# Streaming the activations instead of the second weight matrix in an RWKV-and-FFN kernel

## The chip, the cores and the metric

The kernel runs on one core of one Trainium2 chip. Its time is the device time of one execution in microseconds (us). The metric is the median over the runs; lower is better. All engines of the core take part: TensorE (PE) multiplies, VectorE (DVE), ScalarE (ACT) and GpSimd (POOL) work element by element, and SyncE (SP) issues the transfers between DRAM and the core's memory SBUF. A matmul has a stationary operand of 128 rows and up to 128 columns, which a weight load (PEld) puts into the array, and a moving operand, whose columns stream past it; the result falls into an accumulator bank of PSUM, 128 partitions by 512 float32.

## What is computed

An attention-like recurrence with a state of 48 by 48 for each of 4 batches and 8 heads, over 768 tokens, is followed by a feed-forward layer: 3072 tokens of 384 numbers times `w_in` (384 by 2048), an ELU, and times `w_out` (2048 by 384).

```python
def _attn_ref(r, k, v, w, u):            # B, H, S, D = 4, 8, 768, 48
    state = np.zeros((B, H, D, D))
    for t in range(S):
        kt, vt, rt = (k[:, :, t], v[:, :, t], r[:, :, t])
        cur = np.einsum('bhd,bhe->bhde', u[None] * kt, vt)
        y[:, :, t] = np.einsum('bhd,bhde->bhe', rt, state + cur)
        state = w[None, :, :, None] * state + np.einsum('bhd,bhe->bhde', kt, vt)
    return y

def _moe_ref(x, w_in, w_out):
    h = x @ w_in
    g = np.where(h > 0.0, h, 1.0 * (np.exp(np.minimum(h, 0.0)) - 1.0))
    return (g @ w_out).astype(np.float32)
```

`reference` runs the first on `r, k, v, w, u`, lays the result out as 3072 rows (batch times token) of 384, and runs the second on it.

## The kernel before

The 768 tokens are cut into six blocks of 128 (`NCH`); a block of the feed-forward layer is the 128 tokens of all four batches, 512 columns (`T`). The 2048 hidden channels are cut into 16 groups of 128 (`NF`). A **step** (n, f) is one block and one group, so there are 96 of them, and `step` issues for each, in the order of the tables `FIRST` (block 0) and `LATER` (the others):

- `hidden` (L1172): nine matmuls of 512 columns, three 128-row pieces of x times three products. Both operands are split into a high and a low part (`xh`, `xl`, `wh`, `wl`), and high-high, high-low and low-high are summed.
- `negative`, `elu`, `split_g` (L1181 to L1195): two activations on ACT, one operation on DVE, a rounding copy on ACT for the high part of g, and a subtraction on DVE for the low part.
- `project` (L1209) for the step two before: g is the stationary operand, one 128 by 128 piece for each batch, and 384 columns of `w_out` stream past it. That is four batches times three products, twelve matmuls, into four accumulators `acc0` to `acc3` (one bank each, one buffer each), which collect the 16 groups of a block.

PE takes its work in the order it is written: `hidden` of this step, some small matmuls of the attention in two steps of four, then `project` of the step two before. The attention of the next block runs in units of one batch, spread over four steps each, beside the feed-forward work of this block. In block 0 the weights are also prepared, step by step (ACT, DVE, and `rest_w` L611 on POOL).

When `project` has finished the last group of a block, `store` runs at the end of that step, which is step f = 1 of the next block. It empties the four accumulators, batches 0 and 2 on ACT (L1224), 1 and 3 on DVE (L1222), into the tile `o` (it lies in the weights' old staging area, so the trace calls it `stage`), and issues four stores of 192 KB on the SP queue (L1226). On DVE the copies stand behind that step's `elu` (L1187), low part (L1195) and reduction (L727). The next block's first `project`, in the following step, may write an accumulator only when its copy has ended.

On the SP queue, which is served in order, a unit has four transfers of turned blocks to DRAM (L641), their way back (L646), the loads of r, k and v (L155, L159), and six small transfers that fill rows of x (L1091). The blocks come from `turn_blocks` (L632), which turns 128 by 512 elements on DVE in pieces of 32 by 32.

The whole schedule is written by hand; nothing reorders it.

Of the kernel before, what the change touches and what calls it, by code (L numbers as in the profile page):

```python
# [8 lines left out]
F32 = mybir.dt.float32  # L9
# [8 lines left out]
P = 128  # L18
B, H, S, D = 4, 8, 768, 48
# [3 lines left out]
NC = DM // P  # L23
NF = DFF // P
NCH = S // P
T = B * P
# [30 lines left out]
class Kernel:  # L57
# [237 lines left out]
    def start(self):  # L295
        nc = self.nc

        t = self.wk.tile([P, 2, X // 2], F32, tag="x", name="raw", bufs=2)
        for b in (2, 3):
            n, at = H * DP, t[:, b - 2, :]  # L300
            self.raw[0, b] = [
                at[:, i * n : (i + 1) * n].rearrange("p (h d) -> p h d", h=H) for i in range(3)
            ]
            self.clear_pads(self.raw[0, b])
        self.begun, self.done = [], set()
        n = 3 * H * DP
        self.tails = [
            t[:, i, n : n + DM].rearrange("p (i c d) -> p i c d", i=2, c=NC) for i in range(2)
        ]
        a = self.wk.tile([P, T], F32, tag="a", name="vd", bufs=1)  # L310
        self.vds = [
            t.rearrange("p (c i d) -> p c i d", c=NC, i=2)
            for t in (a[:, 0:DM], self.wide[:, 0].bitcast(F32))
        ]
        for t in self.tails:
            nc.gpsimd.memset(t[:, :, :, 0:D], 0.0)
        dve = nc.vector
        ops = {
            "ub": lambda b: self.u_by_tokens(),
            "inv": lambda b: self.inverse_table(),  # L320
            "kt": lambda b: self.inverse_by_tokens(),
            "wm": lambda b: self.keep_warm(b),
            "Tr": lambda b: self.turn_in(0, b, "r"),
            "Tk": lambda b: self.turn_in(0, b, "k"),
            "dr": lambda b: self.decay_r(0, b),
            "dk": lambda b: self.decay_k(0, b),
            "A": lambda b: self.scores(0, b),
            "ru": lambda b: self.current(0, b),
            "sum": lambda b: self.current_sum(0, b),
            "Lr": lambda b: self.load_rk(0, b, (0,)),  # L330
            "Lk": lambda b: self.load_rk(0, b, (1,)),
            "Ln": lambda b: self.load_next(b),
            "tk": lambda b: self.take_k(0, b, dve.tensor_copy),
            "tka": lambda b: self.take_k(0, b, nc.scalar.copy),
            "uw": lambda b: self.current_by_channels(),
            "p": lambda b: self.current_turned(0, b, dve),
            "pp": lambda b: self.current_turned(0, b, nc.gpsimd),
            "q": lambda b: self.current_by_pe(0, b),
            "qa": lambda b: self.take_current(0, b, nc.scalar.copy),
            "qd": lambda b: self.take_current(0, b, dve.tensor_copy),  # L340
            "ht": lambda b: self.half_tables(),
            "tl": lambda b: self.copy_tails(0, b, nc.gpsimd.tensor_copy),
            "tla": lambda b: self.copy_tails(0, b, nc.scalar.copy),
            "tld": lambda b: self.copy_tails(0, b, dve.tensor_copy),
            "Lv": lambda b: self.load_v(0, b),
            "Lw": lambda b: self.load_weights(b),
            "kr": lambda b: self.key_rest(0, b),
            "krd": lambda b: self.key_rest(0, b, dve),
            "m0": lambda b: self.mask_scores(0, b, 0),
            "m1": lambda b: self.mask_scores(0, b, 1),  # L350
            "m0a": lambda b: self.mask_scores(0, b, 0, True),
            "m1a": lambda b: self.mask_scores(0, b, 1, True),
            "vd": lambda b: self.current_by_v(0, b),
            "vdd": lambda b: self.current_by_v(0, b, dve),
            "O": lambda b: self.output_by_channels(0, b),
            "V": lambda b: self.output_of_current(0, b),
            "xh": lambda b: self.split_output(0, b, 0),
            "xl": lambda b: self.split_output(0, b, 1),
            "dra": lambda b: self.decay_r(0, b, True),
            "dka": lambda b: self.decay_k(0, b, True),  # L360
            "rud": lambda b: self.current(0, b, dve),
            "rsd": lambda b: self.rest_w((b + 1) // 2, (b + 1) % 2, dve),
            "S": lambda b: self.first_state(b),
            "wd": lambda b: self.widen(b),
            "lb": lambda b: self.low_bits(b),
            "ma": lambda b: self.merge(b),
            "mb": lambda b: self.sign(b),
            "sp": lambda b: self.split_w(b),
            "rs": lambda b: self.rest_w((b + 1) // 2, (b + 1) % 2),
            "H": lambda b: self.hidden_half(b),  # L370
        }
        for op in START.split():
            name, _, b = op.partition(":")
            ops[name](int(b or 0))
        self.all_banks = False
# [16 lines left out]
    def step(self, n, f):  # L392
# [64 lines left out]
        for op in (LATER if n else FIRST).split():  # L457
# [3 lines left out]
            name, stage = op[:-1], int(op[-1], 16)  # L461
# [5 lines left out]
                    todo[name](m, b)  # L467
        if last[1] == NF - 1 and last[0] in self.acc:
            self.store(last[0])
        if (n, f) == (0, NF - 1):  # L470

            o = self.late.bitcast(F32).rearrange("p s d w -> p (s d w)")[:, 0 : B * DM]
            self.o = o.rearrange("p (b d) -> p b d", b=B)
# [715 lines left out]
    def split_g(self, n, f, i):  # L1189
# [5 lines left out]
            nc.vector.tensor_sub(part, g, self.g[n, f][2].bitcast(F32))  # L1195
        self.g[n, f].append(part)

    def project(self, n, f):
        gh, gl = self.g.pop((n, f))[2:]
        wh, wl = self.weight(f + 1, 0)  # L1200
        if f == 0:
            self.acc[n] = [
                self.ps.tile([P, 512], F32, tag=f"acc{b}", name=f"ps_acc{b}", bufs=1)
                for b in range(B)
            ]
        for b in range(B):
            at = slice(b * P, (b + 1) * P)
            for i, (a, w) in enumerate(((gh, wh), (gh, wl), (gl, wh))):
                self.nc.tensor.matmul(  # L1209
                    self.acc[n][b][:, 0:DM], lhsT=a[:, at], rhs=w,  # L1210
                    start=(f == 0 and i == 0), stop=(f == NF - 1 and i == 2),
                )

    def store(self, n):
        nc = self.nc
        for b, po in enumerate(self.acc.pop(n)):
            if self.general:
                o = self.wk.tile([P, DM], F32, tag="o", name="o", bufs=2)
            else:
                o = self.o[:, b, :]  # L1220
            if b % 2:
                nc.vector.tensor_copy(o, po[:, 0:DM])  # L1222
            else:
                nc.scalar.copy(o, po[:, 0:DM])  # L1224
            row = b * S + n * P
            nc.sync.dma_start(self.out[row : row + P, :], o)  # L1226
# [43 lines left out]
```

## Time and profile before

| | |
|---|---|
| median of 3 runs | 508.0 us |
| lowest and highest | 507.6 and 509.15 us |
| the profiled execution | 509.15 us, of which the span of the trace is 507.4 us |
| PE, share of the span busy | 97% |
| DVE, ACT, POOL | 56%, 51%, 30% |
| DMA engines, mean rate | 101 GB/s, 39.9% of their time |

The profiled execution is one of the three runs, and the slowest of them. A busy PE is not PE at its peak: each matmul's row lasts until its result is out, and the next one starts before that. So the cost of a matmul in a row of them is the distance from its start to the next start, not the length of its row, and the rows below are read by their starts.

### The profile page before, as it was taken

To read this page: it belongs to the slowest core of one execution; us is meant where nothing else is said; L and a number is where in the kernel's file an instruction comes from. 1 tells how busy PE (TensorE), PEld (TensorE's weight loads), DVE (VectorE), ACT (ScalarE), POOL (GpSimd) and SP (SyncE) were. 2 spreads that over 40 slices of the span, in tenths; PEclk is the share of its full clock that TensorE was granted. 3 is DMA by queue.
4 is the path that set the end of the run, shared out by engine and by line. 5 is a ranking of instruction groups with operands and counts; after the bars stand their busy time and mean duration, and the time that the engine had idled before them with its cause. 6 is when DMAs were issued, how large, how long until landed. Compare 5 with 4: busy or idle time off the path is not lost.

```text
span 507.4 us, 12065 instructions
## 1 busy us (share of the span) xinstructions
PE 491.5 (97%) x4900; PEld 433.4 (85%) x4900; DVE 285.0 (56%) x500; ACT 256.4 (51%) x448; POOL 154.5 (30%) x170
## 2 busy tenths in 40 slices
PE   9899999999999999999999999999999999999994
PEld 7788778888878888888888888888888989999994
DVE  5988989995564454554554653653644533433331
ACT  1458788864544444544444445445435435444441
POOL 3556768683222322312303303313212201000000
PEclk9999999999999999999999999999999999999999
DMA  8986685844533424453423434424443200100002
GB/s 154 236 173 158 154 221 141 178 107 98 166 79 96 123 60 97 107 136 91 113 66 93 122 106 112 110 58 110 102 119 104 76 17 10 62 1 1 1 0 70
DMA packets 105157, 51.10 MB, mean 101 GB/s; under 512 B 79746, under 2 KB 100996, under 8 KB 105092
## 3 DMA queue, kind: packets, MB, share of 16 engines
q1 hardware_dynamic: 105092, 50.23, 39.9%
q8 instruction: 41, 0.67, 0.6%
q14 instruction: 24, 0.20, 0.1%
HBM read 35.13 MB, written 13.11 MB: 95 GB/s over the span
## 4 chain that ended last, share of the span: by engine, by line
PE 75%; POOL 5%; SPq 5%; DMA 5%; DVE 4%; ACT 3%; issue 2%; DVEq 0%; ACTq 0%; POOLq 0%
PE ps_acc L1209 33%; PE ps_h L1172 32%; POOL wl L611 3%; PE ps_y L984 2%; PE ps_a L906 2%; PE ps_y L992 2%; PE ps_a L920 2%; SPq L1091 1%; SPq L201 1%; DMA stage<-in_moe_w_out_dram 1%; POOL k_t L734 1%; DMA raw<-in_v_dram 1%; DVE ps_h L1187 1%; DMA stage<-in_moe_w_in_dram 1%; DMA v_t<-in_v_dram 1%
## 5 line engine op out<-in xcount | busy, mean ns | idle before, releaser
L1209 PE MATMUL ps_acc<-wh,g 128*128 128x384 f32 x768 | 217.1, 343 | 0.4 <-DVE stage L1222 0.2
L1172 PE MATMUL ps_h<-x,wh 128*128 128x512 f32 (+1 forms) x588 | 180.3, 388 | 0.3 <-issue 0.2
L1209 PEld LDWEIGHTS ps_acc<-wh,g 128*128 128x128 f32 x768 | 140.1, 187 | 6.6 <-DVE stage L1222 1.3
L1209 PE MATMUL ps_acc<-wl,g 128*128 128x384 f32 x384 | 129.1, 336 | 0.0
L1187 DVE SCALAR_TENSOR_TENSOR ps_h<-g,ps_h 128x512 f32<-128x512 f32 x96 | 66.6, 694 | 100.8 <-ACT g L1182 100.8
L1172 PEld LDWEIGHTS ps_h<-x,wh 128*128 128x128 f32 x588 | 108.1, 188 | 17.3 <-issue 0.5
L1172 PE MATMUL ps_h<-x,wl 128*128 128x512 f32 (+1 forms) x294 | 115.0, 391 | 2.9 <-POOL wl L611 2.9
L1181 ACT ACTIVATE g<-ps_h 128x512 f32<-128x512 f32 x96 | 57.7, 601 | 87.6 <-PE ps_h L1172 87.5
L1193 ACT CAST g<-ps_h 128x512 fp32r<-128x512 f32 x96 | 56.3, 587 | 75.5 <-DVE ps_h L1187 75.2
L1195 DVE TENSOR_TENSOR g<-ps_h,g 128x512 fp32r<-128x512 f32 x96 | 66.2, 690 | 45.5 <-ACT g L1193 45.1
L1209 PEld LDWEIGHTS ps_acc<-wl,g 128*128 128x128 f32 x384 | 72.1, 188 | 2.1
L1172 PEld LDWEIGHTS ps_h<-x,wl 128*128 128x128 f32 x294 | 55.2, 188 | 16.7 <-POOL wl L611 5.3
L1182 ACT ACTIVATE g<-g 128x512 f32<-128x512 f32 x96 | 60.7, 632 | 3.1
L734 POOL TENSOR_TENSOR k_t<-k_t,rev 128x384 f32<-128x384 f32 x22 | 24.9, 1133 | 103.7 <-DVE ru L716 96.2
L1021 POOL TENSOR_TENSOR x<-x_f,x 128x512 fp32r<-128x512 f32 x16 | 20.7, 1296 | 91.5 <-ACT x L1019 91.5
L611 POOL TENSOR_TENSOR wl<-wide,wh 128x384 fp32r<-128x384 f32 x30 | 37.0, 1250 | 17.7 <-ACT wh L604 14.8
L968 DVE COPY_PREDICATED a<-mask,ps_a 128x256 f32<-128x256 int32 x40 | 17.8, 445 | 33.8 <-PE ps_a L920 32.9
L1003 ACT COPY x_f<-ps_y 128x256 f32<-128x256 f32 x40 | 12.9, 374 | 43.7 <-PE ps_y L992 43.7
L655 POOL TENSOR_TENSOR rk<-rk,pw 128x512 f32<-128x512 f32 x16 | 19.0, 1189 | 36.4 <-DMA rk<-blocks 36.4
L961 POOL TENSOR_TENSOR a<-ident_h,diag 128x512 f32<-128x512 f32 x20 | 21.6, 1080 | 6.7 <-DVE diag L727 5.3
L1012 DVE TENSOR_TENSOR x_f<-x_f,ps_y 128x128 f32<-128x128 f32 x40 | 9.7, 283 | 22.3 <-ACT x_f L1003 22.2
L586 DVE SCALAR_TENSOR_TENSOR wide<-stage 128x768 int32<-128x768 int32 (+1 forms) x17 | 21.5, 1262 | 0.1
(121 smaller groups left out, 416.4 us busy)
## 6 DMA issues: line engine op xcount, KB each, us to landing
blocks<-tb SPq DMA_DIRECT2D x64, 128.0 KB, 2.3
rk<-blocks SPq DMA_DIRECT2D x16, 512.0 KB, 3.5
stage<-in_moe_w_out_dram SPq DMA_DIRECT2D x16, 384.0 KB, 3.9
stage<-in_moe_w_in_dram SPq DMA_DIRECT2D x32, 144.0 KB, 3.8
out_dram<-stage SPq DMA_DIRECT2D x24, 192.0 KB, 2.0
r_t<-in_r_dram SPq DMA_DIRECT2D x22, 192.0 KB, 3.0
k_t<-in_k_dram SPq DMA_DIRECT2D x22, 192.0 KB, 3.6
v_t<-in_v_dram SPq DMA_DIRECT2D x22, 192.0 KB, 4.2
```

Source lines behind the costliest of these rows:

```text
L586: self.nc.vector.scalar_tensor_tensor(self.place(self.wide, k, WIDE), high, 3, low, op0=ALU.logical_shift_left, op1=ALU.bitwise_or,)
L611: (eng or self.nc.gpsimd).tensor_sub(lo, a, hi.bitcast(F32))
L734: (eng or self.nc.gpsimd).tensor_mul(k, k, self.rev[:, :, 0:D])
L961: self.nc.gpsimd.tensor_mul(un["a"], self.ident_h.unsqueeze(1).to_broadcast([P, H, DP]), un["diag"].unsqueeze(2).to_broadcast([P, H, DP]),)
L1021: (eng or nc.gpsimd).tensor_sub(x[:, 1], xf, x[:, 0].bitcast(F32))
L1172: self.nc.tensor.matmul(ph[:, part], lhsT=a[:, c * P : (c + 1) * P], rhs=x[:, c, part], start=(c == 0 and i == 0), stop=(c == NC - 1 and i ...
L1181: nc.scalar.activation(g, ph, AF.Relu, scale=-1.0)
L1182: nc.scalar.activation(g, g, AF.Exp, scale=-1.0)
L1187: self.nc.vector.scalar_tensor_tensor(ph, g, -1.0, ph, op0=ALU.add, op1=ALU.max)
L1193: nc.scalar.copy(part, g)
L1195: nc.vector.tensor_sub(part, g, self.g[n, f][2].bitcast(F32))
L1209: self.nc.tensor.matmul(self.acc[n][b][:, 0:DM], lhsT=a[:, at], rhs=w, start=(f == 0 and i == 0), stop=(f == NF - 1 and i == 2),)
```

## The change

For all blocks but the last (`by_rows`) `project` calls `project_turned`. There `w_out` is the stationary operand and g the moving one: 128 columns of `w_out`, every third one beginning at column c (`w[:, c::NC]`, so that neighbouring elements lie 12 bytes apart), for c = 0, 1, 2, and 512 columns of g. That is three column sets times three products, nine matmuls, into three accumulators, and the result is turned: channels on the partitions, tokens along the bank.

`store` calls `store_turned`: three instructions on DVE turn a bank each, 128 by 512, in blocks of 32 by 32, and write every third element of `o`. ACT has no part in it. After that a partition of `o` holds, for each of 16 groups of 32 tokens, 96 neighbouring channels of one token. The four stores become 16, of 48 KB each in runs of 384 bytes; they are put on a list, and every step issues two from it at its end (`store_pending`), from the step of `store` on. The last block is projected and stored as before.

```diff
+    def by_rows(self, n):
+        return self.general or n + 1 == NCH
+
     def project(self, n, f):
         gh, gl = self.g.pop((n, f))[2:]
         wh, wl = self.weight(f + 1, 0)
+        if not self.by_rows(n):
+            self.project_turned(n, f, gh, gl, wh, wl)
+            return
...
+    def project_turned(self, n, f, gh, gl, wh, wl):
+        if f == 0:
+            self.acc[n] = [
+                self.ps.tile([P, T], F32, tag=f"acc{c}", name=f"ps_acc{c}", bufs=1)
+                for c in range(NC)
+            ]
+        for c in range(NC):
+            for i, (w, g) in enumerate(((wh, gh), (wl, gh), (wh, gl))):
+                self.nc.tensor.matmul(
+                    self.acc[n][c], lhsT=w[:, c::NC], rhs=g,
+                    start=(f == 0 and i == 0), stop=(f == NF - 1 and i == 2),
+                )
+
+    def store_turned(self, n):
+        o = self.o.rearrange("p b d -> p (b d)").rearrange("p (t d c) -> p t d c", t=16, c=NC)
+        for c, po in enumerate(self.acc.pop(n)):
+            self.nc.vector.transpose(o[..., c], po.rearrange("p (t d) -> p t d", t=16))
+        rows = self.out.rearrange("(b n t p) (q d) -> b n t q p d", b=B, n=NCH, p=32, q=4)
+        self.pending = [(rows[b, n, t], o[:, b * 4 + t]) for b in range(B) for t in range(4)]
+
+    def store_pending(self, times):
+        for _ in range(min(times, len(self.pending))):
+            dst, src = self.pending.pop(0)
+            self.nc.sync.dma_start(dst, src.rearrange("p d c -> p (d c)"))
```

On PE, `project` of one step in block 1, before. In the names, `wh5` and `wl5` are the high and low part of a weight group, `g_0` and `g_1` the high and low part of g; the operand behind the arrow's comma is the stationary one:

```order
L1209 MATMUL ps_acc0_1798<-wh5_147,g_0_1964 128x384
L1209 MATMUL ps_acc0_1798<-wl5_148,g_0_1964 128x384
L1209 MATMUL ps_acc0_1798<-wh5_147,g_1_1972 128x384
L1209 MATMUL ps_acc1_1799<-wh5_147,g_0_1964 128x384
L1209 MATMUL ps_acc1_1799<-wl5_148,g_0_1964 128x384
L1209 MATMUL ps_acc1_1799<-wh5_147,g_1_1972 128x384
L1209 MATMUL ps_acc2_1800<-wh5_147,g_0_1964 128x384
L1209 MATMUL ps_acc2_1800<-wl5_148,g_0_1964 128x384
L1209 MATMUL ps_acc2_1800<-wh5_147,g_1_1972 128x384
L1209 MATMUL ps_acc3_1801<-wh5_147,g_0_1964 128x384
L1209 MATMUL ps_acc3_1801<-wl5_148,g_0_1964 128x384
L1209 MATMUL ps_acc3_1801<-wh5_147,g_1_1972 128x384
```

The same on PE in the changed kernel, for the group before it (`wh4`):

```order
L1229 MATMUL ps_acc0_1746<-g_0_1848,wh4_145 128x512
L1229 MATMUL ps_acc0_1746<-g_0_1848,wl4_146 128x512
L1229 MATMUL ps_acc0_1746<-g_1_1851,wh4_145 128x512
L1229 MATMUL ps_acc1_1747<-g_0_1848,wh4_145 128x512
L1229 MATMUL ps_acc1_1747<-g_0_1848,wl4_146 128x512
L1229 MATMUL ps_acc1_1747<-g_1_1851,wh4_145 128x512
L1229 MATMUL ps_acc2_1748<-g_0_1848,wh4_145 128x512
L1229 MATMUL ps_acc2_1748<-g_0_1848,wl4_146 128x512
L1229 MATMUL ps_acc2_1748<-g_1_1851,wh4_145 128x512
```

Twelve matmuls of 384 columns became nine of 512, 4608 columns either way, and the two operands changed sides.

On DVE, around the end of block 1, before: the last turns of attention blocks, an attention addition, `elu`, the low part of g, the reduction, and the two copies of the accumulators.

```order
L632 STREAM_TRANSPOSE tb<-k_t_70 128x4x4x32
L1012 TENSOR_TENSOR x_f<-x_f,ps_y 128x2x64 x2
L1187 SCALAR_TENSOR_TENSOR ps_h<-g,ps_h 128x512
L1195 TENSOR_TENSOR g_2744<-ps_h,g_2734 128x512
L727 TENSOR_REDUCE diag<-ru 128x4x2
L1222 COPY stage<-ps_acc_1799 128x384
L1222 COPY stage<-ps_acc_1801 128x384
L1187 SCALAR_TENSOR_TENSOR ps_h<-g,ps_h 128x512
L1195 TENSOR_TENSOR g_2798<-ps_h,g_2796 128x512
```

The same place on DVE in the changed kernel:

```order
L633 STREAM_TRANSPOSE tb<-k_t_70 128x4x4x32
L1013 TENSOR_TENSOR x_f<-x_f,ps_y 128x2x64 x2
L1188 SCALAR_TENSOR_TENSOR ps_h<-g,ps_h 128x512
L1196 TENSOR_TENSOR g_2657<-ps_h,g_2647 128x512
L728 TENSOR_REDUCE diag<-ru 128x4x2
L1237 STREAM_TRANSPOSE stage<-ps_acc_1746 128x512
L1237 STREAM_TRANSPOSE stage<-ps_acc_1747 128x512
L1237 STREAM_TRANSPOSE stage<-ps_acc_1748 128x512
L1188 SCALAR_TENSOR_TENSOR ps_h<-g,ps_h 128x512
L1196 TENSOR_TENSOR g_2704<-ps_h,g_2702 128x512
```

Two copies became three turns at the same place; the two copies on ACT are gone. On the SP queue, after the end of block 1 in the changed kernel:

```order
L642 DMA blocks<-tb 32x4x256 x4
L647 DMA rk<-blocks 128x1024
L159 DMA v_t_68<-in_v_dram 128x8x48
L1092 DMA x<-x 16x2x128 x6
L1244 DMA out_dram<-stage 4x32x96 x6
L155 DMA r_t_69<-in_r_dram 128x8x48
L155 DMA k_t_70<-in_k_dram 128x8x48
L1244 DMA out_dram<-stage 4x32x96 x2
L642 DMA blocks<-tb 32x4x256 x4
```

Where the six small stores stand, before has its four large ones; the other ten lie behind this and the next unit's loads and x transfers.

## Rows read from the trace of the kernel before

**Rows 1.** The page, busy time of each engine and its share of the span

```profile
PE 491.5 (97%) x4900; PEld 433.4 (85%) x4900; DVE 285.0 (56%) x500; ACT 256.4 (51%) x448; POOL 154.5 (30%) x170
```

**Rows 2.** The page, chain that ended last, by engine

```profile
PE 75%; POOL 5%; SPq 5%; DMA 5%; DVE 4%; ACT 3%; issue 2%; DVEq 0%; ACTq 0%; POOLq 0%
```

**Rows 3.** Busy us of each engine in the stretch 113.75 to 431.17 us

```profile
core 0: us, PE busy (x) PEld busy (x) DVE busy (x) ACT busy (x) POOL busy (x), PEclk, DMA share, GB/s
113.75:431.17 317.42, 315.97 (x3364) 278.01 (x3359) 162.90 (x312) 148.89 (x273) 78.92 (x77) 1.00 0.37 95
```

**Rows 4.** Waits, whole span: who waited for whom; total us, times, longest

```profile
PEld ps_h L1172 <- POOL wl L611: 5.3, 6, 1.2
...
PEld ps_acc L1209 <- DVE stage L1222: 1.3, 3, 0.5
```

**Rows 5.** Timeline of PE, last block: start us, us, instruction, count

```profile
441.64 0.62 PE L1172 MATMUL ps_h<-x,wh 128*128 128x512 f32 x2
...
443.69 0.34 PE L1209 MATMUL ps_acc<-wh,g 128*128 128x384 f32 x1
...
445.78 0.63 PE L1172 MATMUL ps_h<-x,wh 128*128 128x512 f32 x2
...
447.87 0.34 PE L1209 MATMUL ps_acc<-wh,g 128*128 128x384 f32 x1
...
449.98 0.40 PE L1172 MATMUL ps_h<-x,wh 128*128 128x512 f32 x1
```

**Rows 6.** Timeline, last projection of block 1, which follows small matmuls

```profile
205.67 0.19 PEld L1209 LDWEIGHTS ps_acc<-wh,g 128*128 128x128 f32 x1
205.67 0.44 PE L1209 MATMUL ps_acc<-wh,g 128*128 128x384 f32 x1
205.78 0.19 PEld L1209 LDWEIGHTS ps_acc<-wl,g 128*128 128x128 f32 x1
...
207.86 0.63 PE L1172 MATMUL ps_h<-x,wh 128*128 128x512 f32 x2
...
209.94 0.34 PE L1209 MATMUL ps_acc<-wh,g 128*128 128x384 f32 x1
```

**Rows 7.** The same timeline, at the end of block 1

```profile
208.93 0.87 ACT L1224 COPY stage<-ps_acc 128x384 f32<-128x384 f32 x2
...
210.14 1.01 DVE L1222 COPY stage<-ps_acc 128x384 f32<-128x384 f32 x2
...
210.74 0.19 PEld L1209 LDWEIGHTS ps_acc<-wh,g 128*128 128x128 f32 x1 [0.43 <-DVE stage L1222]
```

**Rows 8.** Timelines of DVE and PE at three other block ends

```profile
127.69 1.01 DVE L1222 COPY stage<-ps_acc 128x384 f32<-128x384 f32 x2
...
129.32 0.44 PE L1209 MATMUL ps_acc<-wh,g 128*128 128x384 f32 x1
...
287.56 1.01 DVE L1222 COPY stage<-ps_acc 128x384 f32<-128x384 f32 x2
...
438.79 1.01 DVE L1222 COPY stage<-ps_acc 128x384 f32<-128x384 f32 x2
...
439.52 0.34 PE L1209 MATMUL ps_acc<-wh,g 128*128 128x384 f32 x1
```

**Rows 9.** Timelines of DVE: strided reads, plain reads, 32 by 32 turns

```profile
100.52 1.79 DVE L586 SCALAR_TENSOR_TENSOR wide<-stage 128x768 int32<-128x768 int32 x1
...
200.77 0.55 DVE L715 TENSOR_TENSOR ru<-r_t,u_b 128x384 f32<-128x384 f32 x1
...
204.00 0.70 DVE L632 STREAM_TRANSPOSE tb<-r_t 128x512 f32<-128x512 f32 x1
...
204.63 0.67 DVE L632 STREAM_TRANSPOSE tb<-k_t 128x512 f32<-128x512 f32 x1
```

**Rows 10.** Timeline of the SP queue, end of block 1 and after

```profile
214.63 2.01 SPq L1226 DMA_DIRECT2D out_dram<-stage  x4
...
224.92 1.94 SPq L641 DMA_DIRECT2D blocks<-tb  x4
```

More of the change, by code (lines that the diff above doesn't have):

```diff
@@ L304, in start @@
             self.clear_pads(self.raw[0, b])
-        self.begun, self.done = [], set()
+        self.begun, self.done, self.pending = [], set(), []
         n = 3 * H * DP
@@ L469, in step @@
             self.store(last[0])
+        self.store_pending(2)
         if (n, f) == (0, NF - 1):
@@ L1212, in project @@
                 )
+    def project_turned(self, n, f, gh, gl, wh, wl):
[20 more added lines that the diff above has]
+            self.nc.sync.dma_start(dst, src.rearrange("p d c -> p (d c)"))
     def store(self, n):
+        if not self.by_rows(n):
+            self.store_turned(n)
+            return
         nc = self.nc
```

## The prediction

> **What bounds the kernel now.** I read the page first, then the busy time by stretch, then PE's timeline by starts. PE is busy for 97% of the span, DVE, ACT and POOL for 30 to 56% [rows 1], and the chain that ended last runs through PE for 75% of its length [rows 2]. Once the weights are prepared it is nearly all PE: from 113.75 to 431.17 us, 65 steps, PE is busy for 315.97 of 317.42 us [rows 3]. So in blocks 1 to 4 anything that shortens or lengthens the row of matmuls shows one for one, and what happens on ACT, DVE or SP shows only where PE waits for it. In block 0 PE also waits for POOL's weight parts, 5.3 us of weight loads in six waits [rows 4]; there a shorter `project` only makes that wait longer. I count from about 113 us on: 67 steps of the 80 that the change touches.
>
> **Twelve matmuls against nine.** Both stream 4608 columns a step. The trace has both kinds side by side: `hidden` is nine matmuls of 512 columns, `project` twelve of 384. In the last block, where nothing else is on PE, `hidden` takes 443.69 - 441.64 = 2.05 and 447.87 - 445.78 = 2.09 us, `project` 2.09 and 2.11 us [rows 5]. So nine pieces are 0.02 to 0.04 us cheaper than twelve beside them, 0.03 in the mean. In the projections that follow small attention matmuls, half of all, the first weight load is not covered: the second load starts 205.78 - 205.67 = 0.11 us after it, and the step takes 207.86 - 205.67 = 2.19, so 2.08 without that; the `hidden` behind it takes 209.94 - 207.86 = 2.08 [rows 6]. There nothing is gained. Mean over the two kinds: about 0.015 us a step; I take 0.02, since the dearest `project` and the cheapest `hidden` differ by 0.06. Sum: 67 x 0.02 = 1.3 us gained. Bounds: 67 x 0 = 0, and 67 x 0.06 = 4.0 us. The gain is small because the price goes with the columns, 2.10 / 12 = 0.175 us for 384 and 2.07 / 9 = 0.230 for 512, not with the count.
>
> **Weights read at every third element.** The new stationary operand lies at steps of 12 bytes; PE has no such load in the trace. A plain one takes 0.11 us when uncovered [rows 6], and the matmul ahead of it, now 0.23 us long, covers it unless it gets more than twice as slow. The nearest strided reads are DVE's, of every second word: the slowest took 1.79 us for 768 elements, 2.33 ns each, against 0.55 us for 384 plain ones, 1.43 ns each, a factor of 1.63, with POOL at work at the same time [rows 9]. At that factor a load takes 0.18 us: still covered, but in the 34 projections after small matmuls it stands bare, 34 x 0.07 = 2.4 us. Bounds 0 and 2.4; I take 0, because the plain loads have as much cover again as they need.
>
> [...]
>
> **The end of a block.** Before, ACT copies two banks early (208.93 us) and DVE the other two from 210.14 us on; PE wants its second accumulator before that copy is done and its weight load waits 0.43 us, until 210.74 [rows 7]. Three block ends look like this (blocks 1, 2 and 3), 1.3 us of waiting in all [rows 4], which the change takes away. After the change ACT's copies are gone, and with them the bank that was free early. All three banks wait for DVE, whose work before them is unchanged, so the first turn starts at the same 210.14 us. A turn of 128 by 512 takes 0.70 us, the next starts 0.63 us later [rows 9]. The first bank is free at 210.84 us, plus 0.05 as between copy and load today; the first matmul would have started at 209.94 [rows 6]: 0.95 us lost, plus 0.10 for the load behind a wait, 1.05 us. After that PE spends 3 x 0.23 = 0.69 us on each bank, a little more than DVE on the next turn, and doesn't wait again. Cost: 3 x 1.05 - 1.3 = 1.9 us. At the end of block 0 the turns start at 127.69 us and PE comes at 129.32: nothing. At the end of block 4 they start at 438.79 us, the first bank is free at 439.54, PE comes at 439.52 [rows 8], and the twelve matmuls of the last block go faster through a bank (0.52 us) than DVE: some 0.3 us. Sum: 2.2 us lost. Below: if the turns run no slower than a copy of three quarters the size, 0.2 us less at each of the four, 1.4 us. Above: turns slowed by the 1.63 of the strided read, 1.14 us each, would lose 0.44 us more at the first bank and 0.33 at each later one, 1.1 us at three block ends, some 1.1 at the two others: 6.6 us.
>
> What is queued behind the turns on DVE: the next `elu`, low part of g, attention additions, all about 1 us later once a block (three turns take 1.96 us, the two copies 1.01). g is projected two steps, over 8 us, after it is made; the cover is ample.
>
> **The small stores.** 80 stores take the place of 20. One issue takes about 0.5 us of SP's time (four in 2.01 us [rows 10]). Six come where four stood, so the loads behind them are late by 1 us once a block; before the next unit's blocks the queue stands idle until 224.92 us, when DVE has turned them [rows 10], so this cover is several us. PE waits for no store, and `o` is free again eight steps before it is needed. Cost 0; without that cover it would be 1 us at each of five block ends, 5 us.
>
> **The sum.** -1.3 + 0 + 2.2 + 0 = +0.9 us. The profiled execution would go from 509.15 to 510.05 us (a span of 508.3 for 507.4); it lay 1.15 us above the median, so against the median of 508.0 us: **508.9 us**.
>
> **The rivals.**
> First, **strided access is slow** (slower). Loads of 0.18 us stand bare in 34 places, +2.4, and turns of 1.14 us make the block ends cost 6.6 instead of 2.2, +4.4: 508.9 + 6.8 = 515.7 us; one of the two effects alone, 511.3 or 513.3. It decides on a measurable loss from 0.6 us on, 0.02 us a load in those places. Beyond 0.23 us a load each further 0.01 us costs 9 x 0.01 x 67 = 6 us: then it would be 520 and more. [...]
> Second, **the nine matmuls run like the cheapest hidden step** (faster). One moving operand serves all three banks, and each `project` drops from 2.11 to 2.05 us: -4.0, with block ends at 1.4: 508.0 - 4.0 + 1.4 = 505.4 us. For it: `hidden` has such steps in each pair [rows 5]. Against it: after small matmuls both kinds take 2.08 us [rows 6].
> Third, **the SP queue fills up**: the stores push the r, k and v loads and the x transfers until PE waits, +1 us at each of five block ends: 513.9 us. Against it: the idle time before 224.92 us.
> Fourth, the change does nothing that PE feels: the terms cancel, 508.0 us; it lies inside the forecast's range.
>
> **How the numbers follow.** This measurement can tell 0.3%, 1.5 us, from no change. The forecast with its cancelling terms, 506.5 to 510.5 us, has a chance of 0.45: of that 0.32 within 1.5 us of 508.0, 0.11 slower, 0.02 faster. Strided access 0.24, all slower. The cheap nine 0.24: 0.20 faster, 0.04 within. The full SP queue 0.07: 0.03 slower, 0.04 within, since part of it may be covered. Together: faster 0.22, same 0.40, slower 0.38. The range of eight in ten takes in the second rival almost whole and of the first all but its far half: 505.2 to 514.5 us.
>
> **What would show it.** In the timeline of PE the distance from the first `project` matmul to the next `hidden`: 2.05 to 2.09 us in steps without small matmuls; below 2.05 the second rival holds, above 2.12 the first. After small matmuls, the distance of the first two weight loads: 0.11 us, or 0.18. On DVE the turns of the banks: 0.70 us each, 0.63 apart; about 1.1 us for the first rival. At the ends of blocks 1 to 3 a wait of PE for DVE's turn of 0.9 to 1.0 us, and none at the end of block 0. In the SP queue no wait of PE that leads to a load. I would be wrong if nine matmuls came out much cheaper than `hidden` at the same width, if the turns ran at another price than those of SBUF, or if PE waited at block ends for something other than the first bank.

## The result: 1% slower, and where the time went

The changed kernel takes 513.74 us in the median (512.85 to 514.04) beside 507.98 us before: 5.8 us more between the medians; the ratio on record is 1.010, interval 1.0085 to 1.0114, so the loss is known to about 1 us. PE is as full as before, so the loss is to be looked for in PE's own row of work. The page's busy line, which answers to [rows 1], and its two groups of weight loads (line, operation, shape, count, then busy us and mean ns of one):

```profile
PE 495.1 (97%) x4660; PEld 435.3 (85%) x4660; DVE 290.8 (57%) x505; ACT 253.0 (50%) x438; POOL 153.9 (30%) x170
...
L1173 PEld LDWEIGHTS ps_h<-x,wh 128*128 128x128 f32 x588 | 109.3, 188 | 19.8 <-issue 0.5
L1229 PEld LDWEIGHTS ps_acc<-g,wh 128*128 128x128 f32 x480 | 118.0, 252 | 8.1 <-ACT g L1182 4.1
```

There are 240 fewer matmuls and loads. A load of `hidden` still has a row of 188 ns; one of the new `project` has 252, 64 ns more. Not all of a row lies in PE's way, so the starts decide. The timeline of the last projection of block 1, which follows small matmuls, as in [rows 6]:

```profile
205.53 0.25 PEld L1229 LDWEIGHTS ps_acc<-g,wh 128*128 128x128 f32 x1
205.53 0.57 PE L1229 MATMUL ps_acc<-g,wh 128*128 128x512 f32 x1
205.69 0.26 PEld L1229 LDWEIGHTS ps_acc<-g,wl 128*128 128x128 f32 x1
...
207.82 0.63 PE L1173 MATMUL ps_h<-x,wh 128*128 128x512 f32 x2
```

The second load starts 0.16 us after the first, 0.11 before; the projection takes 207.82 - 205.53 = 2.29 us where it took 2.19. A projection that follows `hidden` directly, where every load has cover (timeline of PE in block 4):

```profile
412.27 0.39 PE L1229 MATMUL ps_acc<-g,wh 128*128 128x512 f32 x1
...
414.37 0.63 PE L1173 MATMUL ps_h<-x,wh 128*128 128x512 f32 x2
```

2.10 us, against 2.09 and 2.11 in [rows 5]: next to nothing gained. And the end of block 1, as in [rows 7] (timeline of DVE, PEld and PE):

```profile
207.82 0.63 PE L1173 MATMUL ps_h<-x,wh 128*128 128x512 f32 x2
...
210.03 2.29 DVE L1237 STREAM_TRANSPOSE stage<-ps_acc 128x512 f32<-128x512 f32 x3
...
211.01 0.25 PEld L1229 LDWEIGHTS ps_acc<-g,wh 128*128 128x128 f32 x1 [1.39 <-ACT g L1182]
211.04 0.54 PE L1229 MATMUL ps_acc<-g,wh 128*128 128x512 f32 x1 [0.99 <-DVE stage L1237]
...
211.42 0.40 PE L1229 MATMUL ps_acc<-g,wl 128*128 128x512 f32 x1
```

From `hidden` to the first matmul of the next block go 211.04 - 207.82 = 3.22 us instead of 2.08, and the second matmul follows after 0.38 instead of 0.23. Over the whole span PE waits for the turns as follows (waits: who for whom, total us, times, longest); they answer to the second row of [rows 4]:

```profile
PE ps_acc L1229 <- DVE stage L1237: 2.9, 3, 1.0
...
PEld ps_acc L1216 <- DVE stage L1237: 0.4, 2, 0.2
```

The sum by these rows, for the 67 steps once the weights are prepared: 32 of the projections follow small matmuls and cost 32 x 0.10 = 3.2 us more. The three block ends cost 3 x (1.14 + 0.15) = 3.9 us and the end of block 4 some 0.3, where before they cost 1.3: 2.9 us more. The other 35 projections give back about 0.4 us. Together 5.7 us.

PE's starts say the same without a sum. From the first projection of block 1 to the second of block 5 PE needed 443.69 - 129.32 = 314.37 us before ([rows 8], [rows 5]), and in the changed kernel 449.06 - 128.84 = 320.22, 5.85 us more:

```profile
128.84 0.57 PE L1229 MATMUL ps_acc<-g,wh 128*128 128x512 f32 x1
...
449.06 0.34 PE L1216 MATMUL ps_acc<-wh,g 128*128 128x384 f32 x1
```

The spans of the two traces, 507.4 and 511.1 us, differ by 3.7 us only, because two other stretches went the other way: the one ahead of this was 0.5 us shorter in the changed kernel's trace, and after PE's last matmul had started the profiled execution before took another 7.5 us, this one 5.9. That end is the same work in both kernels; in the runs below it took between 5.6 and 6.7 us.

### The profile page after: what moved, and what is told of

Read it like the earlier page. It is cut to its first block, busy times and chain, and to the rows that moved or that the text cites. A ratio compares the mean times of both kernels' runs of the same rounds, so it can differ in the third digit from the quotient of the medians.

```text
span 511.1 us, 11635 instructions
## 1 busy us (share of the span) xinstructions
PE 495.1 (97%) x4660; PEld 435.3 (85%) x4660; DVE 290.8 (57%) x505; ACT 253.0 (50%) x438; POOL 153.9 (30%) x170
## 4 chain that ended last, share of the span: by engine, by line
PE 78%; DVE 6%; DMA 5%; ACT 4%; POOL 2%; SPq 2%; issue 2%; DVEq 0%; ACTq 0%; POOLq 0%
PE ps_h L1173 33%; PE ps_acc L1229 29%; PE ps_acc L1216 7%; PE ps_y L985 2%; PE ps_a L907 2%; PE ps_y L993 2%; DMA stage<-in_moe_w_in_dram 2%; PE ps_a L921 2%; DMA stage<-in_moe_w_out_dram 1%; POOL wl L612 1%; SPq L1092 1%; DVE ps_h L1188 1%; DMA v_t<-in_v_dram 1%; ACT g L1183 1%; DVE wide L587 1%
## 5 line engine op out<-in xcount | busy, mean ns | idle before, releaser
L1229 PE MATMUL ps_acc<-g,wh 128*128 128x512 f32 x480 | 172.3, 413 | 2.9 <-DVE stage L1237 2.9
L1173 PEld LDWEIGHTS ps_h<-x,wh 128*128 128x128 f32 x588 | 109.3, 188 | 19.8 <-issue 0.5
L1229 PEld LDWEIGHTS ps_acc<-g,wh 128*128 128x128 f32 x480 | 118.0, 252 | 8.1 <-ACT g L1182 4.1
L1229 PE MATMUL ps_acc<-g,wl 128*128 128x512 f32 x240 | 95.5, 398 | 0.0
L1229 PEld LDWEIGHTS ps_acc<-g,wl 128*128 128x128 f32 x240 | 60.8, 253 | 0.0
L1216 PE MATMUL ps_acc<-wh,g 128*128 128x384 f32 x128 | 35.4, 339 | 0.1
L1216 PEld LDWEIGHTS ps_acc<-wh,g 128*128 128x128 f32 x128 | 23.4, 187 | 1.5 <-issue 0.5
```

The costliest lines, as they stand in the source:

```text
L1173: self.nc.tensor.matmul(ph[:, part], lhsT=a[:, c * P : (c + 1) * P], rhs=x[:, c, part], start=(c == 0 and i == 0), stop=(c == NC - 1 and i ...
L1216: self.nc.tensor.matmul(self.acc[n][b][:, 0:DM], lhsT=a[:, at], rhs=w, start=(f == 0 and i == 0), stop=(f == NF - 1 and i == 2),)
L1229: self.nc.tensor.matmul(self.acc[n][c], lhsT=w[:, c::NC], rhs=g, start=(f == 0 and i == 0), stop=(f == NF - 1 and i == 2),)
```

## Experiments

The theory A after these rows: reading `w_out` at steps of 12 bytes makes a weight load slow, which shows where a load has no cover; and all banks waiting for one engine costs the rest at block ends. The rivals: loads are slow because the operands changed sides; the turns, 0.83 us each, are slow because they read PSUM; what is queued behind the turns costs, not the bank; the small stores hold up SP. The first four kernels below were timed beside the kernel before at 508.6 us, the other four beside it at 508.11 us.

**Neighbouring columns as the stationary operand.**

```diff
-                    self.acc[n][c], lhsT=w[:, c::NC], rhs=g,
+                    self.acc[n][c], lhsT=w[:, c * P : (c + 1) * P], rhs=g,
```

> The changed kernel with one edit: the stationary operand is 128 neighbouring columns of w_out instead of every third one. Turns, stores and their order stay, so the columns of the output of blocks 0 to 4 are permuted. Theory A (the step of 12 bytes makes the weight loads slow): the uncovered first load of the 33 projections after small matmuls falls from 0.17 to 0.11 us, matmuls from 0.235 to 0.230 us, a projection after small matmuls from 2.29 to 2.18 us, others from 2.10 to 2.07; 33 x 0.11 + 35 x 0.03 = 4.7 us less, 509.0 us. Theory B (loads of w_out are slow whatever their step, because the operands changed sides): the load row stays at 252 ns, 513.7 us.

Measured: 509.07 us, ratio to the kernel before 1.001 (1.0001 to 1.002). The same place in its timeline, and its group of loads:

```profile
204.18 0.19 PEld L1229 LDWEIGHTS ps_acc<-g,wh 128*128 128x128 f32 x1
204.19 0.50 PE L1229 MATMUL ps_acc<-g,wh 128*128 128x512 f32 x1
204.29 0.19 PEld L1229 LDWEIGHTS ps_acc<-g,wl 128*128 128x128 f32 x1
...
206.36 0.63 PE L1173 MATMUL ps_h<-x,wh 128*128 128x512 f32 x2
```

```profile
L1229 PEld LDWEIGHTS ps_acc<-g,wh 128*128 128x128 f32 x480 | 90.0, 188 | 25.8 <-ACT g L1182 4.4 <-DVE g L1196 0.3
```

The load is back at 188 ns and 0.11 us, the projection at 2.18 us. The step alone is worth 4.7 us of the 5.8 by the medians, 4.1 by PE's starts (table below): theory A, and the operands' sides have no part in it. That is more than the bare loads, 32 x 0.06 = 1.9 us: covered matmuls get faster too. By PE's starts 4.1 - 32 x 0.11 = 0.6 us are left for the 35 covered projections, some 0.02 us each, from 2.10 to 2.08 us.

**Turns that write runs of 32.** `o` is laid out with c ahead of d, and each turn writes 32 neighbouring elements.

```diff
-        o = self.o.rearrange("p b d -> p (b d)").rearrange("p (t d c) -> p t d c", t=16, c=NC)
+        o = self.o.rearrange("p b d -> p (b d)").rearrange("p (t c d) -> p t c d", t=16, c=NC)
...
-            self.nc.vector.transpose(o[..., c], po.rearrange("p (t d) -> p t d", t=16))
+            self.nc.vector.transpose(o[:, :, c, :], po.rearrange("p (t d) -> p t d", t=16))
...
```

> The changed kernel with one edit: the turns write runs of 32 neighbouring elements instead of every third one; loads and stores stay, so the columns of the output of blocks 0 to 4 are permuted. Theory A (strided writes slow the turns): a turn falls from 0.85 to 0.70 us and starts 0.63 instead of 0.73 us after the last, PE's wait at four block ends is 0.15 us shorter: 0.6 us less, 513.1 us. Theory B (the turn is slow because it reads PSUM): 0.85 us stays, 513.7 us.

Measured: 512.21 us, ratio 1.0073 (1.0059 to 1.0087). The instructions of the turns' line (min/median/max ns, first and last start), in the changed kernel:

```profile
L1237 DVE STREAM_TRANSPOSE stage<-ps_acc x15: 801/830/867, 127.1 to 445.0; 128x512 f32<-128x512 f32 x15
```

and here, with who waited for it:

```profile
L1237 DVE STREAM_TRANSPOSE stage<-ps_acc x15: 672/674/707, 127.7 to 445.4; 128x512 f32<-128x512 f32 x15
...
  PE ps_acc L1229: 2.4, 3
```

The strided write cost a turn 0.16 us, 830 against 674 ns, and PSUM as the source cost nothing: 674 ns is what the turns in SBUF took, 0.70 and 0.67 us [rows 9]. PE's wait falls from 2.9 to 2.4 us. The time fell by about 1.5 us, more than these 0.5, but the intervals of this kernel and of the changed one overlap a little, and PE's starts show 0.3 us; the wait is what is shown.

**Accumulators that go round four banks.** The last block's four, projected as before, go round with them.

```diff
...
-                self.ps.tile([P, T], F32, tag=f"acc{c}", name=f"ps_acc{c}", bufs=1)
+                self.ps.tile([P, T], F32, tag=f"acc{(n * NC + c) % 4}", name=f"ps_acc{(n * NC + c) % 4}", bufs=1)
...
```

> The changed kernel with one edit: the three accumulators of a block go round the four banks, so that the first bank of the next block is always free. Theory A (PE's wait for the first turned bank is what a block end costs): PE does three matmuls, 0.70 us, before it needs a turned bank; the wait of 1.26 us at blocks 1 to 3 falls to 0.5 and the 0.3 at block 4 goes: 3 x 0.75 + 0.3 = 2.6 us less, 511.1 us. Theory B (the block end is dear because elu and the attention are queued behind three turns on DVE): the gap moves elsewhere, 513.7 us.

Measured: 510.42 us, ratio 1.0039 (1.0025 to 1.0053), 3.3 us less than the changed kernel (2.8 by PE's starts). Its timeline at the end of block 1:

```profile
210.48 0.39 PE L1229 MATMUL ps_acc<-g,wh 128*128 128x512 f32 x1
...
210.62 2.27 DVE L1237 STREAM_TRANSPOSE stage<-ps_acc 128x512 f32<-128x512 f32 x3
...
211.53 0.25 PEld L1229 LDWEIGHTS ps_acc<-g,wh 128*128 128x128 f32 x1 [0.56 <-DVE stage L1237]
```

PE starts the next block before DVE starts the first turn, and waits 0.56 us later on instead of 0.99 at once with 0.38 behind it. What stands behind the turns on DVE is as late as ever, `elu` 2.16 us after the first turn's start beside 2.17 in the changed kernel, and PE does not feel it: theory A.

**No small stores.** The changed kernel clears the list instead of issuing from it.

```diff
-        self.store_pending(2)
+        self.pending.clear()
```

> The changed kernel without the 80 small stores (the output of blocks 0 to 4 is left unwritten); all else stays. Theory A (PE waits for no store, SP's idle time covers their issue): 513.7 us, within 1 us. Theory B (80 stores at 0.54 us each on the SP queue make loads and x transfers late): 1 us at each of five block ends, 508.7 us.

Measured: 513.44 us, ratio 1.0093 (1.0077 to 1.0108), 0.3 us from the changed kernel and inside the noise; PE's starts span 320.20 us where they spanned 320.22 with the stores. The stores cost PE nothing. In the changed kernel's SP queue, the place of [rows 10]:

```profile
215.26 3.57 SPq L1244 DMA_DIRECT2D out_dram<-stage  x6
218.88 0.49 SPq L155 DMA_DIRECT2D r_t<-in_r_dram  x1
220.88 0.37 SPq L155 DMA_DIRECT2D k_t<-in_k_dram  x1
```

Six issues take 3.57 us and end at 218.83; the four large ones ended at 214.63 + 2.01 = 216.64. The load of r starts behind them, and still the queue stands idle ahead of the load of k, from 219.37 to 220.88 us.

**All three edits.** Plain loads, plain writes and four banks; the stores put the rows right in runs of 128 bytes.

```diff
...
+        rows = self.out.rearrange("(b n t p) (c q d) -> b n t q p c d", b=B, n=NCH, p=32, c=NC, q=4)
...
```

> The changed kernel with all three edits at once: neighbouring columns of w_out as the stationary operand, turns that write runs of 32, accumulators that go round four banks; the stores put the rows in their places in runs of 128 bytes. Theory A (the loads' step and the wait for the first turned bank are the loss, and they are separate places on PE): the gains add, 513.7 - 4.7 - 3.3 - 0.5 = 505.2 us, faster than the kernel before. Theory B (they are not separate, or runs of 128 bytes make the stores slow enough to be waited for): 508 us or more.

Measured: 505.77 us, ratio 0.9949 (0.9933 to 0.9964), 0.5% faster than the kernel before. The gains add, to within 0.6 us of what was expected. What is left of the wait:

```profile
PEld ps_acc L1229 <- DVE stage L1237: 1.7, 3, 0.6
```

**The same, with the turns ahead of the reduction on DVE.**

```diff
+            if op == "sum5" and last[1] == NF - 1 and last[0] in self.acc:
+                self.store(last[0])
...
```

> The same as the kernel with all three edits, and the three turns stand ahead of the reduction on DVE instead of behind it, 0.46 us earlier. Theory A (PE waits for the end of the first turn): the 0.3 us that are left of the wait at the ends of blocks 1 to 3 go as well, 504.4 us. Theory B (what is left is the load behind a wait, not the turn): no difference, 505.2 us.

Measured: 505.13 us, ratio 0.9937 (0.9919 to 0.9954). Its timeline at the end of block 1:

```profile
208.85 1.90 DVE L1239 STREAM_TRANSPOSE stage<-ps_acc 128x512 f32<-128x512 f32 x3
209.06 0.40 PE L1231 MATMUL ps_acc<-g,wh 128*128 128x512 f32 x1
...
209.99 0.40 PE L1231 MATMUL ps_acc<-g,wl 128*128 128x512 f32 x1
```

The first matmul of each bank finds it free, nine starts in the 2.09 us to the next `hidden`, and the wait is gone from the list of waits; in time the two kernels differ by 0.6 us, and their intervals overlap, so the trace shows it and the times don't.

**Two other steps of the load, for their price.** Each was timed once, and in both the output of blocks 0 to 4 is not what the reference computes. In the first the stationary operand is every second column of `w_out`, steps of 8 bytes; all else is as in the changed kernel.

```diff
-                    self.acc[n][c], lhsT=w[:, c::NC], rhs=g,
+                    self.acc[n][c], lhsT=w[:, c % 2 : c % 2 + 2 * P : 2], rhs=g,
```

> [...] Theory B (any step above one element slows the load): load row 252 ns, 513.7 us.

Measured: 510.43 us, below the 513.7 of theory B and above every one of the plain loads' executions (508.0 to 509.97). Its loads (min/median/max ns), and the last projection of block 1:

```profile
L1229 PEld LDWEIGHTS ps_acc<-g,wh x480: 192/194/198, 42.8 to 439.5; 128*128 128x128 f32 x160
...
204.85 0.51 PE L1229 MATMUL ps_acc<-g,wh 128*128 128x512 f32 x1
...
207.06 0.63 PE L1173 MATMUL ps_h<-x,wh 128*128 128x512 f32 x2
```

The projection takes 2.21 us, 0.03 more than with plain loads, of which a bare load's 6 ns are the smaller part; by PE's starts the step of two costs 2.0 us.

In the second the stationary operand is, in 15 of 16 steps, every fourth column of a pair of weight groups, steps of 16 bytes.

```diff
+                w = w[:, c::NC]
+                if f + 1 < NF:
+                    pair = self.pairs[f + 1][i == 1].rearrange("p a d -> p (a d)")
+                    w = pair[:, c : c + 4 * P : 4]
...
```

> [...] Theory B (a step is a step): load row 252 ns, 513.7 us.

Measured: 515.72 us. Its loads:

```profile
L1233 PEld LDWEIGHTS ps_acc<-g,wh x480: 251/309/334, 42.6 to 444.7; 128*128 128x128 f32 x160
```

Steps of one, two, three and four elements have rows of 188, 194, 252 and 309 ns: two adds 6 ns, three 64, four 121. Theory B, 252 ns at either step, holds for neither. At a step of two the row is nearly the plain one, and PE still loses 2.0 us. Added to the plain load's 0.11 us, the rows give 0.17 for three and 0.23 for four, 1.6 and 2.1 times; by the start of the second load it is 0.16 and 0.21, 1.5 and 2.0 times. What sets these prices, and whether they go on rising with the step, is not shown: no step beyond four was run.

PE's starts in all these kernels, over the stretch from the first projection of block 1 to the second of block 5, in us:

| kernel | from | to | takes |
|---|---|---|---|
| before | 129.32 | 443.69 | 314.37 |
| changed | 128.84 | 449.06 | 320.22 |
| neighbouring columns | 128.56 | 444.65 | 316.09 |
| every second column | 128.76 | 446.86 | 318.10 |
| every fourth column | 128.95 | 451.99 | 323.04 |
| turns that write runs of 32 | 129.44 | 449.33 | 319.89 |
| four banks | 129.41 | 446.84 | 317.43 |
| no small stores | 129.06 | 449.26 | 320.20 |
| all three edits | 128.57 | 441.00 | 312.43 |
| and the turns earlier | 129.19 | 440.42 | 311.23 |

## Why the prediction came out as it did

The range, 505.2 to 514.5 us, held 513.74. The forecast inside it, 508.9 us by terms that nearly cancel, did not come; what came is the first rival, strided access, between its 511.3 and 515.7 us, to which I had given 0.24. Even there the total is luck: the rival had 2.4 us for the loads and 4.4 for slow turns, and the loads cost 4.7 us, the slow turns 0.5 us of PE's wait. So the range held because it was drawn wide enough to take in that rival, and the working behind the forecast failed in one step.

- **Twelve against nine: -1.3 us forecast, about -0.4 measured**, in the projections that follow `hidden`. The reading behind it was right: matmuls cost by their columns here, 2.10 / 12 = 0.175 us for 384 and 2.08 / 9 = 0.231 for 512 with plain loads, and the plain-load run shows what was there to gain, 2.11 to 2.08 us and 2.19 to 2.18, some 1.4 us. The strided loads ate it.
- **Strided loads: 0 taken, 2.4 the upper bound. This is the step that failed.** I took 0 "because the plain loads have as much cover again as they need", after writing in the same passage that 34 projections have a first load without cover (the trace has 32). Cover says nothing there. The bare loads cost 32 x 0.06 = 1.9 us. The whole projection around such a load took 0.11 us more than with plain loads, and the covered ones 0.02 to 0.03, because covered matmuls went slower too, which no term had. All together the step cost 4.7 us, about twice the bound. For the same reason the first rival's limit was wrong, that a load has to pass 0.23 us before covered matmuls pay: they paid at 0.17.
- The factor of 1.63 that gave the bound came near the load's 1.5 to 1.6 by chance. Its row, 1.79 us [rows 9], stands near the dear end of 15 rows of one instruction, 0.95 to 1.80 us, and the stride is not what made it dear. With the same stride and size the instruction took 0.95 us when POOL was idle, 1.24 ns for each element, less than the plain row's 1.43:

```profile
47.78 0.95 DVE L586 SCALAR_TENSOR_TENSOR wide<-stage 128x768 int32<-128x768 int32 x1
```

All its rows above 1.2 us had POOL at work beside them, but so had two of 0.95 and 0.96 us. That POOL made them dear is my estimate from these rows; no run tried it.

- **Block ends: +2.2 us forecast, +2.9 measured.** The mechanism, the places and their order held: the first bank alone, three block ends and a little at the fourth, none at block 0. Mis-sized was the turn: 0.83 us and 0.73 apart instead of 0.70 and 0.63, by the strided write, not by PSUM. The load and matmul behind the wait cost 0.15 us where 0.10 was taken.
- **Stores: 0 forecast, 0 measured** (without them 513.44 us). The third rival is out. So is the second: covered projections stayed at 2.10 us, and even with plain loads they come to 2.08, not 2.05.
- **Behind the turns on DVE: nothing**, as forecast; four banks took most of the wait away and left that queue alone.

## What to carry to other kernels

Before a stride is put on an operand, find the places where its load has no cover and price those; an average over covered places hides them (here 32 places, at 0.11 us a projection). Don't take the covered places as free either: here they were more than half of the 4.7 us. If turning a result round makes one engine empty all accumulators, spend a spare bank so that the next block can start ahead of that engine: here it took 3.3 us off the time. The swap of stationary and moving operands at equal columns gained little here: 2 to 3 us with every stride removed and the spare bank used.

## What the runs showed that I had not expected

Here strided loads slowed matmuls that they lay wholly beside. With loads of 0.17 us under matmuls of 0.23 us a projection took 2.10 instead of 2.08 us, and the nine matmuls after the bare load lost 2.29 - 2.18 - 0.06 = 0.05 us. Even a step of two elements, whose load is 6 ns longer, lost some 0.02 us in this way, 2.21 - 2.18 - 0.006, in the projection shown above. Nothing in these runs says by which path. And a DVE turn of a PSUM bank was no dearer than one in SBUF: 674 ns against 0.67 and 0.70 us [rows 9].
